# Scores of the last 64 queries of a head pair in four 64x64 tiles, with keys and values regrouped around their middle 64

## The chip, the cores and the metric

The kernel runs on one core of a Trainium2 chip. The metric is the time of one execution on the device in microseconds (us): the median of several runs.

## What is computed

Threshold attention over 8 batches, 8 heads, 576 positions and a head size of 64, followed by a Fourier mixing layer and a two-layer MLP with ReLU (512 to 2048 to 512). All data are 32-bit floats.

```python
scores = (1 / sqrt(64)) * q @ k.T                        # 8 x 8 x 576 x 576
thresh = max(scores, axis=-1) - tau
scores = where(scores >= thresh, scores, -1e9)
attn = exp(scores - max(scores, axis=-1))
attn = attn / (sum(attn, axis=-1) + 1e-9)
x = (attn @ v).transpose(0, 2, 1, 3).reshape(8, 576, 512)
u = x + real(fft(fft(x, axis=1), axis=2))
un = (u - mean(u)) / sqrt(var(u) + 1e-6)                 # over the last axis
out = u + maximum(un @ w_ch1, 0) @ w_ch2
```

## The kernel before

**Pairs and steps.** The 64 heads are worked on two at a time: 32 *pairs* n, four to a batch. The two heads of a pair lie above each other, head j = 0 on partitions 0 to 63, head j = 1 on 64 to 127. A pair has five *steps* t; the running number is i = 5n + t. In steps 0 to 3, 128 queries of each head are treated; in step 4, the *ends step*, the last 64 queries of both heads. 576 is four and a half times 128, so both queries and keys leave 64 over; that is what the change is about.

**Making ready.** `load_pair` loads q and k of a pair, `prep_pair` turns them in DVE's 32x32 transposes into `kT` and `qT` (64 rows of head size per head; lines 408, 409 and 411). `kT` has 64 columns in front that hold, for head 1 alone, its last 64 keys once more (L409), so that head 1 can read its keys rotated: the last 64 first, then 0 to 511. `scale_q` scales the raw q on ACT. `prep_ends` copies the last 64 query columns of both heads on GpSimd (L420) into `q_ends`, a 128x128 tile that is zero elsewhere: block-diagonal, head 0 in the first 64 rows and columns, head 1 in the others.

**Scores.** `scores(i)` writes into PSUM tiles `sc` of two banks each (two such tiles exist). In steps 0 to 3 each head has a tile with 288 keys in each bank; its matmuls use only the head's 64 rows of TensorE (64x128 tiles, L440), so the two heads can run beside each other. In the ends step two full-size matmuls (L446) of 128 rows with `q_ends` as the weights give one tile: 64 queries of head 0 on partitions 0 to 63 and of head 1 on the others, each against all 576 keys.

**Softmax.** DVE finds the row maximum, negated (`neg`, L461 in the first eight pairs, L520 later); ACT forms the exponential `e` (L477, L526) and the threshold `thr` (L530); DVE zeroes what lies under it and sums the rest (L540, denominators in `den_eps`); `inverse` adds up the denominators and takes the reciprocal (L385, L388). In an ends step all these are one instruction over 128 rows of 576 where the other steps need two. From pair 8 on ACT multiplies `e` with the reciprocal (L549); before that the reciprocals are carried along (`rec`, `spread_inverse`) and applied to the result of the values.

**Weights and values.** `weights_in_parts(i - 1)` transposes the previous step's `e` on TensorE and copies it out of PSUM on ACT. Columns 512 to 639 of `e` are the last 64 keys of head 0 followed by the last 64 keys of head 1: one 128x128 transpose (`pe`, L587) serves both, and goes to `ends` (L593; in an ends step two copies, L597). In the ends step, which has one head's width only, L504 or L554 first copies columns 512 to 575 to 576 to 639, so that both halves of the transpose hold them. The other 4 x 128 keys of each head are the transposes `pw` (L605) with copies to `e_t` (L607, L609). `values_in_parts` multiplies with v: five pairs of column-tiled matmuls (L636) into `pv`, four with `e_t`, the fifth with `ends`, whose v has zeros where the other head's keys stand. `load_v` brings v: `vt[:, 2c + j]` holds keys 128c to 128c + 127 of head j (c < 4), `vt[64j:64j+64, 8 + j]` its last 64, in four transfers on SP's queue.

**Three stretches.** Pairs 0 to 3 (`step`, with one `softmax` call per step; TensorE also prepares w1), pairs 4 to 7 (`second_batch`), and pairs 8 to 31 (the late loop), where a step's softmax is cut into `softmax_first`, `softmax_second` and `softmax_third` with pieces of the MLP and of the mixing of an earlier batch (`fill`, `mix`) between them. The order of each engine's instructions is what the program writes out, line by line. In the late loop it is, for an ends step: `scores` on TensorE; `softmax_first` (maximum, exponential, threshold); `fill`; `softmax_second` (mask, denominators); sometimes a part of the mixing; `weights_in_parts` of step 3; `fill`; `softmax_third`; `fill`; `load_pair`. `prep_pair` of the next pair stands at the end of step 3, just ahead of the ends step, and its transposes are thus ahead of the ends step's maximum on DVE. `prep_ends` stands at step 1, `load_v` at step 2.

**The work around it.** The MLP's two products are done by a two-level Strassen scheme: L1210 (first product, `ph`) and L1400 (second, `po`), 128x128 weights. L1147 and L1152 (DVE, ACT) evacuate `ph`, L1420 (DVE) adds `po` up, L1156, L1168, L1191, L1263 and L1346 are sums on GpSimd or DVE. The Fourier mixing of a batch: column sums and folds (L296, L299, L376), L766 (products `py`) with copies on ACT (L771, L776), L783 and L787 (products over the heads' dimension) into `f`. In the late loop it stands beside the first pair of the next batch. PSUM outside `sc` is a ring of four one-bank tiles (tag `mm`) that L1210, L1400, `pe`, `pw`, `pv` and `py` share in the order of the program: a tile comes free when its evacuation, on ACT or DVE, is done. w, hs and f are also moved to and from the device's main memory on SP's queue (L1074 among them), and L134 there loads q and k.

Of the kernel before, what the change touches and what calls it, by code (L numbers as in the profile page):

```python
# [9 lines left out]
FP32 = mybir.dt.float32  # L10
# [37 lines left out]
def kernel(  # L48
# [94 lines left out]
    def load_v(n):  # L143

        b, p = n // NPAIR, PAIRS[n % NPAIR]
        vt = v_in[n % 2]
        for j in range(2):
            h = 2 * p + (j + p) % 2
            nc.sync.dma_start(
                out=vt[:, j:8:2, :], in_=v[b, h, 0:512, :].rearrange("(t p) d -> p t d", p=128)  # L150
            )
            nc.sync.dma_start(out=vt[64 * j : 64 * j + 64, 8 + j, :], in_=v[b, h, 512:576, :])
# [15 lines left out]


    q_ends = const.tile([128, 128], FP32, name="q_ends")  # L170
    nc.gpsimd.memset(q_ends[:, :], 0.0)
# [211 lines left out]
    def inverse(i, nh):  # L383
        den = sb.tile([128, 2], FP32, tag="den", bufs=3, name="den")
        nc.vector.tensor_reduce(  # L385
            out=den[:, 0:nh], in_=den_eps[i % 3][:, 0:nh, :], axis=AXIS_X, op=ALU.add
        )
        nc.vector.reciprocal(den[:, 0:nh], den[:, 0:nh])  # L388
        return den

    heads = {}
    steps = {}
    xs = {}
# [7 lines left out]
    def prep_pair(n):  # L401
# [5 lines left out]
        kT = sb.tile([128, D + S], FP32, tag="kT", name="kT")  # L407
        nc.vector.transpose(kT[:, D : D + S], k_raw[:, :])
        nc.vector.transpose(kT[64:128, 0:D], k_raw[64:128, 512:S])  # L409
# [5 lines left out]

    def prep_ends(n):

        for j in range(2):
            hp = slice(64 * j, 64 * j + 64)
            nc.gpsimd.tensor_copy(q_ends[hp, hp], heads[n][0][hp, 512:S])  # L420
# [6 lines left out]
    def scores(i):  # L427
# [3 lines left out]
        nh = 2 if t < 4 else 1  # L431
        sc = [ps.tile([128, 2, 512], FP32, tag="sc", name=f"sc{j}") for j in range(nh)]
        if t < 4:
            order = [(c, j) for c in range(2) for j in range(2)]
            if i < per_batch:
                order.sort(key=lambda cj: cj[1])
            for c, j in order:
                if True:
                    hp, k0 = slice(64 * j, 64 * j + 64), D * (1 - j)
                    nc.tensor.matmul(  # L440
                        sc[j][:, c, 0:HALF], qT[hp, 128 * t : 128 * t + 128],
                        kT[hp, k0 + HALF * c : k0 + HALF * (c + 1)], start=True, stop=True,
                    )
        else:
            for c in range(2):
                nc.tensor.matmul(  # L446
                    sc[0][:, c, 0:HALF], q_ends[:, :], kT[:, D + HALF * c : D + HALF * (c + 1)],
                    start=True, stop=True,
                )
        steps[i] = (sc, nh)  # L450

    def softmax(i, between=None, meanwhile=None, behind=None):


        t = i % NT
        sc, nh = steps[i]
        neg = sb.tile([128, 2], FP32, tag="neg", bufs=3, name="neg")
        thr = sb.tile([128, 2], FP32, tag="thr", bufs=3, name="thr")
        e = sb.tile([128, 2 * S], FP32, tag="e", name="e")
        for j in range(nh):  # L460
            nc.vector.tensor_reduce(  # L461
                out=neg[:, j : j + 1], in_=sc[j][:, :, 0:HALF], axis=AXIS_XY, op=ALU.max,
                negate=True,
            )
        if meanwhile is not None:
            meanwhile()
        for j in range(nh):
            ej = e[:, S * j : S * (j + 1)].rearrange("p (c n) -> p c n", c=2)
            nc.scalar.activation(
                out=ej, in_=sc[j][:, :, 0:HALF], func=ACT.Exp, bias=neg[:, j : j + 1], scale=1.0  # L470
            )
            if j == 0:
                nc.scalar.activation(
                    out=thr[:, 0:nh], in_=neg[:, 0:nh], func=ACT.Identity,
# [1435 lines left out]
```

## Time and profile before

| What | us |
| --- | --- |
| median of 3 runs | 1545.07 (1543.23 to 1547.54) |
| the profiled execution: its own time | 1547.94 |
| its span, first to last instruction | 1546.2 |
| mean granted TensorE clock in it | 0.997 |

The profile is of one execution. Its busy times by stretch (us of the engine within each stretch; the first ends with pair 3, the second with pair 7, the third with pair 31, the last is the rest of the MLP):

| stretch, us | length | PE | DVE | ACT | POOL | DMA share |
| --- | --- | --- | --- | --- | --- | --- |
| 0 to 160 | 160 | 149.1 | 127.3 | 110.1 | 95.9 | 0.44 |
| 160 to 300 | 140 | 138.1 | 106.1 | 95.0 | 56.0 | 0.40 |
| 300 to 1340 | 1040 | 1036.1 | 718.0 | 655.7 | 514.6 | 0.52 |
| 1340 to 1546 | 206 | 200.6 | 111.7 | 55.6 | 112.8 | 0.58 |

PE is TensorE's matmuls, DVE VectorE, ACT ScalarE, POOL GpSimd, SP the engine that issues most transfers. Lines such as L446 are lines of the kernel. A line of the page's list of groups gives line, engine, operation, output<-input with sizes, count, then busy time, mean duration in ns, and the idle time just before such instructions with what ended most of it. Matmuls are pipelined and their ends are modelled, so that a matmul's duration contains time in which the one before it still ran: the distance between starts is the firmer number.

### The profile page before, as it was taken

To read this page: it belongs to the slowest core of one execution; us is meant where nothing else is said; L and a number is where in the kernel's file an instruction comes from. 1 tells how busy PE (TensorE), PEld (TensorE's weight loads), DVE (VectorE), ACT (ScalarE), POOL (GpSimd) and SP (SyncE) were. 2 spreads that over 40 slices of the span, in tenths; PEclk is the share of its full clock that TensorE was granted. 3 is DMA by queue.
4 is the path that set the end of the run, shared out by engine and by line. 5 is a ranking of instruction groups with operands and counts; after the bars stand their busy time and mean duration, and the time that the engine had idled before them with its cause. 6 is when DMAs were issued, how large, how long until landed. Compare 5 with 4: busy or idle time off the path is not lost.

```text
span 1546.2 us, 27021 instructions
## 1 busy us (share of the span) xinstructions
PE 1524.0 (99%) x9786; PEld 1186.0 (77%) x9786; DVE 1063.2 (69%) x2141; ACT 916.4 (59%) x1921; POOL 779.4 (50%) x964
## 2 busy tenths in 40 slices
PE   9999999999999999999999999999999999999999
PEld 5556555556788778887788878887788778989999
DVE  7977676846779466866578566956687657746546
ACT  6875676655666576656775666666665676133131
POOL 3775563034365642546255724554264625647635
PEclk9999999999999999999999999999999999999999
DMA  7423233465956354644455354635464534646655
GB/s 171 130 59 119 78 92 105 139 183 165 280 187 206 92 173 125 186 113 146 146 167 160 120 159 133 199 92 172 120 195 132 160 117 142 220 163 231 234 196 184
DMA packets 248907, 239.31 MB, mean 155 GB/s; under 512 B 197027, under 2 KB 218533, under 8 KB 228678
## 3 DMA queue, kind: packets, MB, share of 16 engines
q1 hardware_dynamic: 246262, 237.28, 50.1%
q8 instruction: 78, 1.28, 0.3%
q10 hardware_dynamic: 2512, 0.30, 0.1%
q14 instruction: 55, 0.45, 0.1%
HBM read 205.93 MB, written 31.46 MB: 154 GB/s over the span
## 4 chain that ended last, share of the span: by engine, by line
PE 91%; DVE 4%; ACT 2%; POOL 1%; DMA 1%; issue 0%; ACTq 0%; DVEq 0%; POOLq 0%
PE ph L1210 25%; PE po L1400 21%; PE pv L636 10%; PE sc L440 10%; PE pw L605 7%; PE po L933 4%; PE ph L909 3%; PE sc L446 2%; PE py L766 2%; PE pe L587 1%; PE pa L783 1%; PE pn L858 1%; PE pa L787 1%; PE pm L360 1%; PE po L1379 1%; DVE neg L461 1%
## 5 line engine op out<-in xcount | busy, mean ns | idle before, releaser
L520 DVE TENSOR_REDUCE neg<-sc 128x1 f32<-128x576 f32 x216 | 154.3, 751 | 117.1 <-PE sc L440 105.5
L526 ACT ACTIVATE e<-sc,neg 128x576 f32<-128x576 f32 x216 | 158.6, 734 | 114.3 <-DVE neg L520 114.3
L1147 DVE TENSOR_TENSOR hs<-ph,hs 128x512 f32<-128x512 f32 (+1 forms) x128 | 105.3, 823 | 167.1 <-PE ph L1210 97.3
L1400 PE MATMUL po<-w,w_all 128*128 128x128 f32 x1728 | 219.4, 276 | 0.0
L1400 PEld LDWEIGHTS po<-w,w_all 128*128 128x128 f32 x1728 | 205.4, 192 | 7.4 <-issue 4.0
L1156 POOL TENSOR_TENSOR w<-hs 128x512 f32<-128x512 f32 x32 | 42.1, 1317 | 312.3 <-ACT hs L1152 249.3
L540 DVE SCALAR_TENSOR_TENSOR e<-sc,thr,e 128x576 f32<-128x576 f32 x216 | 168.4, 812 | 27.2 <-ACT thr L530 27.1
L1210 PE MATMUL ph<-u_t,w 128*128 128x256 f32 x768 | 180.9, 382 | 0.6 <-DMA w<-f 0.6
L607 ACT COPY e_t<-pw 128x512 f32<-128x512 f32 x256 | 148.4, 594 | 44.2 <-PE pw L605 42.7
L440 PE MATMUL sc<-kT,qT 64*128 64x288 f32 x1024 | 168.4, 430 | 5.9 <-DVE e L477 5.5
L605 PE MATMUL pw<-ident,e 128*128 128x128 f32 x1152 | 169.3, 274 | 3.7 <-ACT ends L593 1.9
L549 ACT ACTIVATE e<-e,den 128x576 f32<-128x576 f32 x216 | 157.4, 774 | 2.9 <-DVE den L388 2.2
L1210 PEld LDWEIGHTS ph<-u_t,w 128*128 128x128 f32 x768 | 140.9, 190 | 23.6 <-issue 5.3
L1210 PE MATMUL ph<-w_all,w 128*128 128x256 f32 x672 | 157.1, 382 | 1.1 <-DVE w_all L1132 1.0
L605 PEld LDWEIGHTS pw<-ident,e 128*128 128x128 f32 x1152 | 135.8, 141 | 19.3 <-issue 5.6
L1263 POOL TENSOR_TENSOR w_all<-w_all 128x128 f32<-128x128 f32 (+2 forms) x160 | 121.7, 777 | 44.5 <-DVE w_all L1420 23.4
L1210 PEld LDWEIGHTS ph<-w_all,w 128*128 128x128 f32 x672 | 123.5, 190 | 23.9 <-issue 4.9
L1152 ACT ACTIVATE hs<-hs 128x512 f32<-128x512 f32 (+1 forms) x96 | 74.1, 772 | 113.8 <-DVE hs L1147 113.0
L440 PEld LDWEIGHTS sc<-kT,qT 64*128 64x128 f32 x1024 | 95.1, 186 | 55.4 <-issue 22.9
L1400 PE MATMUL po<-w,hs 128*128 128x128 f32 x912 | 119.8, 278 | 0.0
L1400 PEld LDWEIGHTS po<-w,hs 128*128 128x128 f32 x912 | 109.8, 192 | 9.5 <-issue 8.0
L636 PE MATMUL pv<-e_t,v_in 128*64 128x320 f32 (+1 forms) x512 | 72.1, 423 | 1.5 <-ACT e_t L609 0.8
(227 smaller groups left out, 2910.6 us busy)
## 6 DMA issues: line engine op xcount, KB each, us to landing
w<-f SPq DMA_DIRECT2D x150, 1024.0 KB, 4.9
hs<-in_moe_w_ch_dram SPq DMA_DIRECT2D x23, 512.0 KB, 4.7
q_in<-in_q_dram SPq DMA_DIRECT2D x128, 72.0 KB, 4.1
out_dram<-u SPq DMA_DIRECT2D x36, 256.0 KB, 2.5
k_in<-in_k_dram SPq DMA_DIRECT2D x124, 72.0 KB, 2.4
v_in<-in_v_dram SPq DMA_DIRECT2D x64, 128.0 KB, 5.1
f<-w SPq DMA_DIRECT2D x14, 512.0 KB, 3.3
f<-w SPq DMA_DIRECT2D x7, 1024.0 KB, 4.8
```

The costliest lines, as they stand in the source:

```text
L440: nc.tensor.matmul(sc[j][:, c, 0:HALF], qT[hp, 128 * t : 128 * t + 128], kT[hp, k0 + HALF * c : k0 + HALF * (c + 1)], start=True, stop=True,)
L520: nc.vector.tensor_reduce(out=neg[:, j : j + 1], in_=sc[j][:, :, 0:HALF], axis=AXIS_XY, op=ALU.max, negate=True,)
L526: nc.scalar.activation(out=ej, in_=sc[j][:, :, 0:HALF], func=ACT.Exp, bias=neg[:, j : j + 1], scale=1.0)
L540: nc.vector.scalar_tensor_tensor(out=ej, in0=sc[j][:, :, 0:HALF], scalar=thr[:, j : j + 1], in1=ej, op0=ALU.is_ge, op1=ALU.mult, accum_out ...
L549: nc.scalar.activation(out=e[:, S * j : S * (j + 1)], in_=e[:, S * j : S * (j + 1)], func=ACT.Copy, scale=den[:, j : j + 1],)
L605: nc.tensor.transpose(pw[:, c, :], e[:, c0 : c0 + 128], ident[:, :])
L607: nc.scalar.copy(e_t[:, 4 * j : 4 * j + 4, qs], pw[:, :, :])
L636: nc.tensor.matmul(pv[64 * j : 64 * j + 64, 0:m], vt[:, 2 * c + j, :], e_t[:, 4 * j + c, 0:m] if c < 4 else ends[:, 0, 0:m], start=(c == 0 ...
L1147: nc.vector.tensor_tensor(out=to, in0=bank, in1=to if other is None else other, op=ALU.add)
L1210: nc.tensor.matmul(bank[:, 256 * q : 256 * q + 256].rearrange("p (two n) -> p two n", two=2), left[:, 256 * c + 128 * q : 256 * c + 128 * ...
L1263: return lambda: eng.tensor_tensor(out=to, in0=to, in1=other, op=ALU.add)
L1400: nc.tensor.matmul(to, lefts[m][j][:, s], right_[:, 128 * s : 128 * (s + 1)], start=jn in (0, 4) and s == 0, stop=s == 3, skip_group_check ...
```

## The change

Three things, which go together:

- **The odd 64 keys are now those in the middle** (256 to 319) and no longer the last. `kT` is laid out as keys 256 to 575, 32 columns with a half of the middle 64 (another half for each head), then keys 0 to 319: 672 columns in four transposes. In steps 0 to 3 head 0 reads its keys as 320 to 575 and 0 to 319, head 1 as 256 to 575 and 0 to 255, cut into matmuls of 256 and 320 columns where both were 288; in PSUM the two pieces meet at the end of the first bank, so that the 576 are one run. The middle keys of both heads again stand beside each other in `e`, at 512 to 639. `load_v` brings the 512 other keys in two transfers for each head instead of one, and the middle 64 in a third.
- **The ends step's scores are four 64x64 tiles**: head j (rows of TensorE) times half c of its keys (columns, so partitions 64c to 64c + 63 of the output), 288 columns each; head j goes to bank j. `q_ends`, its memset and `prep_ends` are gone. Each row of the output now holds half the keys of one query of one head, in bank j.
- **The ends step's softmax follows that layout.** One maximum over both banks gives two numbers for each row (`own`); `exchange` copies them between the two halves of the partitions (two copies), and their minimum is `neg`. Exponential, mask and scaling are two instructions of 288 columns where one had 576; the denominators are exchanged between the halves as well, into a third column that `inverse` adds. `e` is 576 columns wide in that step; `pe` is the transpose of columns 256 to 383, and `ends` is filled by four copies of 32 partitions; `L504` and `L554` are gone.

The instructions that `softmax`, `softmax_first`, `softmax_second` and `softmax_third` had inline for the maximum, the exponential and the mask are moved into functions (`maxima`, `exponentials`, `masked`, `weights_of`).

```diff
@@ -146,10 +146,12 @@
         vt = v_in[n % 2]
         for j in range(2):
             h = 2 * p + (j + p) % 2
-            nc.sync.dma_start(
-                out=vt[:, j:8:2, :], in_=v[b, h, 0:512, :].rearrange("(t p) d -> p t d", p=128)
-            )
-            nc.sync.dma_start(out=vt[64 * j : 64 * j + 64, 8 + j, :], in_=v[b, h, 512:576, :])
+            for first, k0 in ((0, 320), (2, 0)):
+                nc.sync.dma_start(
+                    out=vt[:, first + j : 8 : 4, :],
+                    in_=v[b, h, k0 : k0 + 256, :].rearrange("(t p) d -> p t d", p=128),
+                )
+            nc.sync.dma_start(out=vt[64 * j : 64 * j + 64, 8 + j, :], in_=v[b, h, 256:320, :])
     tau_t = const.tile([128, 1], FP32, name="tau_t")
     nc.scalar.dma_start(out=tau_t[:, :], in_=tau.partition_broadcast(128))
...
-    q_ends = const.tile([128, 128], FP32, name="q_ends")
-    nc.gpsimd.memset(q_ends[:, :], 0.0)
...
@@ -380,16 +378,24 @@
     for den in den_eps:
         nc.vector.memset(den[:, :, :], 1e-9)
-    def inverse(i, nh):
+    den_ends = const.tile([128, 2, 3], FP32, name="den_ends")
+    nc.vector.memset(den_ends[:, :, :], 1e-9)
+    own = const.tile([128, 2], FP32, name="own")
+    other = const.tile([128, 2], FP32, name="other")
+
+    def inverse(i):
         den = sb.tile([128, 2], FP32, tag="den", bufs=3, name="den")
-        nc.vector.tensor_reduce(
-            out=den[:, 0:nh], in_=den_eps[i % 3][:, 0:nh, :], axis=AXIS_X, op=ALU.add
-        )
-        nc.vector.reciprocal(den[:, 0:nh], den[:, 0:nh])
+        parts = den_eps[i % 3]
+        if i % NT == 4:
+            parts = den_ends
+            exchange(parts[:, :, 2], parts[:, :, 0])
+        nc.vector.tensor_reduce(out=den[:, :], in_=parts[:, :, :], axis=AXIS_X, op=ALU.add)
+        nc.vector.reciprocal(den[:, :], den[:, :])
         return den
     heads = {}
     steps = {}
+    begun = {}
     xs = {}
     sums = {}
@@ -404,21 +410,18 @@
         q_raw, k_raw = loaded.pop(n)
-        kT = sb.tile([128, D + S], FP32, tag="kT", name="kT")
-        nc.vector.transpose(kT[:, D : D + S], k_raw[:, :])
-        nc.vector.transpose(kT[64:128, 0:D], k_raw[64:128, 512:S])
+        kT = sb.tile([128, S + 96], FP32, tag="kT", name="kT")
+        nc.vector.transpose(kT[:, 0:320], k_raw[:, 256:S])
+        nc.vector.transpose(kT[:, 352:672], k_raw[:, 0:320])
+        for j, k0 in ((0, 288), (1, 256)):
+            hp = slice(64 * j, 64 * j + 64)
+            nc.vector.transpose(kT[hp, 320:352], k_raw[hp, k0 : k0 + 32])
         qT = sb.tile([128, S], FP32, tag="qT", bufs=1, name="qT")
         nc.vector.transpose(qT[:, :], q_raw[:, :])
         heads[n] = (qT, kT, v_in[n % 2])
         if n + 1 < B * NPAIR and not late:
             load_pair(n + 1)
-    def prep_ends(n):
-
-        for j in range(2):
-            hp = slice(64 * j, 64 * j + 64)
-            nc.gpsimd.tensor_copy(q_ends[hp, hp], heads[n][0][hp, 512:S])
-
     def normalized(n):
-        sc = [ps.tile([128, 2, 512], FP32, tag="sc", name=f"sc{j}") for j in range(nh)]
+        sc = [
+            ps.tile([128, 2, 512], FP32, tag="sc", name=f"sc{j}") for j in range(2 if t < 4 else 1)
+        ]
+        order = [(c, j) for c in range(2) for j in range(2)]
+        if i < per_batch and t < 4:
+            order.sort(key=lambda cj: cj[1])
+        for c, j in order:
+            hp = slice(64 * j, 64 * j + 64)
+            if t < 4:
+                k0, k1 = ((64, 320), (352, 672), (0, 320), (352, 608))[2 * j + c]
+                to = sc[j][:, c, 512 - (k1 - k0) : 512] if c == 0 else sc[j][:, c, 0 : k1 - k0]
+                q_cols = slice(128 * t, 128 * t + 128)
+            else:
+                k0, k1 = ((64, 352), (352, 640), (32, 320), (320, 608))[2 * j + c]
+                to, q_cols = sc[0][64 * c : 64 * c + 64, j, 0:HALF], slice(512, S)
+            nc.tensor.matmul(
+                to, qT[hp, q_cols], kT[hp, k0:k1], start=True, stop=True, skip_group_check=t == 4
+            )
         if t < 4:
-            order = [(c, j) for c in range(2) for j in range(2)]
-            if i < per_batch:
-                order.sort(key=lambda cj: cj[1])
-            for c, j in order:
-                if True:
-                    hp, k0 = slice(64 * j, 64 * j + 64), D * (1 - j)
-                    nc.tensor.matmul(
-                        sc[j][:, c, 0:HALF], qT[hp, 128 * t : 128 * t + 128],
-                        kT[hp, k0 + HALF * c : k0 + HALF * (c + 1)], start=True, stop=True,
-                    )
+            steps[i] = [
+                sc[j][:, :, :].rearrange("p c n -> p (c n)")[:, 256 - 64 * j : 832 - 64 * j]
+                for j in range(2)
+            ]
         else:
-            for c in range(2):
-                nc.tensor.matmul(
-                    sc[0][:, c, 0:HALF], q_ends[:, :], kT[:, D + HALF * c : D + HALF * (c + 1)],
-                    start=True, stop=True,
+            steps[i] = [sc[0][:, j, 0:HALF] for j in range(2)]
+
+    def weights_of(i, e, j):
+
+        if i % NT == 4:
+            return e[:, HALF * j : HALF * (j + 1)]
+        return e[:, S * j : S * (j + 1)]
+
+    def maxima(i):
+        neg = sb.tile([128, 2], FP32, tag="neg", bufs=3, name="neg")
+        sc = steps[i]
+        if i % NT < 4:
+            for j in range(2):
+                nc.vector.tensor_reduce(
+                    out=neg[:, j : j + 1], in_=sc[j], axis=AXIS_X, op=ALU.max, negate=True
                 )
-        steps[i] = (sc, nh)
+            return neg
+        both = bass.AP(
+            tensor=sc[0].tensor, offset=sc[0].offset,
+            ap=[list(sc[0].ap[0]), [512, 2], list(sc[0].ap[1])],
+        )
+        nc.vector.tensor_reduce(
+            out=own[:, :], in_=both, axis=AXIS_X, op=ALU.max, negate=True
+        )
+        exchange(other[:, :], own[:, :])
+        nc.vector.tensor_tensor(out=neg[:, :], in0=own[:, :], in1=other[:, :], op=ALU.min)
+        return neg
+
+    def exchange(out_, in_):
+
+        for half in range(2):
+            a, b = 64 * half, 64 - 64 * half
+            nc.vector.tensor_copy(out_[a : a + 64], in_[b : b + 64])
+
+    def exponentials(i, e, neg, thr, j):
+        nc.scalar.activation(
+            out=weights_of(i, e, j), in_=steps[i][j], func=ACT.Exp, bias=neg[:, j : j + 1],
+            scale=1.0,
+        )
+        if j == 0:
+            nc.scalar.activation(
+                out=thr[:, :], in_=neg[:, :], func=ACT.Identity, bias=thr_off[:, :], scale=-1.0
+            )
+
+    def masked(i, e, thr, j):
+        ej = weights_of(i, e, j)
+        nc.vector.scalar_tensor_tensor(
+            out=ej, in0=steps[i][j], scalar=thr[:, j : j + 1], in1=ej, op0=ALU.is_ge,
+            op1=ALU.mult, accum_out=(den_ends if i % NT == 4 else den_eps[i % 3])[:, j, 0:1],
+        )
     def softmax(i, between=None, meanwhile=None, behind=None):
-        t = i % NT
...
     def spread_inverse(i):
         e, den = steps[i]
-        if i % NT == 4:
-            nc.scalar.copy(e[:, S : S + 64], e[:, 512:S])
         if den is None:
             return
-        nh = den.shape[1]
+        nc.scalar.copy(rec[:, :].rearrange("p (j d) -> p j d", j=2), _repeated(den, D))
...
     def softmax_first(i):
+        neg = maxima(i)
...
+        for j in range(2):
+            exponentials(i, e, neg, thr, j)
...
     def softmax_second(i):
...
+        e, thr = begun.pop(i)
+        for j in range(2):
+            masked(i, e, thr, j)
+        steps[i] = (e, inverse(i))
...
     def softmax_third(i):
...
-        if nh == 1:
-            nc.scalar.copy(e[:, S : S + 64], e[:, 512:S])
+        e, den = steps[i]
+        for j in range(2):
+            ej = weights_of(i, e, j)
+            nc.scalar.activation(out=ej, in_=ej, func=ACT.Copy, scale=den[:, j : j + 1])
...
-        nc.tensor.transpose(pe[:, 0, :], e[:, 512:640], ident[:, :])
+        c0 = 512 if t < 4 else 256
+        nc.tensor.transpose(pe[:, 0, :], e[:, c0 : c0 + 128], ident[:, :])
         kept = 1
...
             for j in range(2):
-                hp = slice(64 * j, 64 * j + 64)
-                nc.scalar.copy(ends[hp, 0:kept, q0 : q0 + 64], pe[hp, 0:kept, hp])
+                for half in range(2):
+                    p0 = 64 * j + 32 * (1 - half)
+                    nc.scalar.copy(
+                        ends[p0 : p0 + 32, 0, q0 : q0 + 64],
+                        pe[32 * j : 32 * j + 32, 0, 64 * half : 64 * half + 64],
+                    )
+            if kept == 2:
+                nc.scalar.copy(ends[:, 1, q0 : q0 + 64], pe[:, 1, 0:64])
         qs = slice(q0, q0 + (128 if t < 4 else 64))
         for j in range(2 if t < 4 else 1):
             pw = ps.tile([128, 4, 128], FP32, tag="mm", bufs=4, name="pw")
             if j == 1:
                 yield
             for c in range(4):
-                c0 = (S + D) * j + 128 * c
+                if t < 4:
+                    c0 = (S + D) * j + 256 * (c % 2) + 128 * (c // 2)
+                else:
+                    c0 = 320 * (c // 2) + 128 * (c % 2)
                 nc.tensor.transpose(pw[:, c, :], e[:, c0 : c0 + 128], ident[:, :])
             if t < 4:
                 nc.scalar.copy(e_t[:, 4 * j : 4 * j + 4, qs], pw[:, :, :])
             else:
                 nc.scalar.copy(
-                    e_t[:, :, qs].rearrange("p (j c) q -> p j c q", j=2),
-                    pw[:, :, :].rearrange("p c (j q) -> p j c q", j=2),
+                    e_t[:, :, qs], pw[:, :, :].rearrange("p c (two q) -> p (c two) q", two=2)
                 )
     def values_in_parts(n, part):
...
-        if t == 1:
-            prep_ends(n)
         if i > 0:
             transposed_weights(i - 1)
         spread_inverse(i)
```

The calls of `prep_ends` in the other two stretches go as well.

## The prediction

> **What bounds the kernel now.** I read the page's busy shares and its chain first, then the timeline of TensorE around each kind of score step, then, for every place where TensorE resumes after a score step of a pair's last 64 queries (an "ends step", 32 of them), what it waits for and since when that was ready.
>
> ```profile
> PE 1524.0 (99%) x9786; PEld 1186.0 (77%) x9786; DVE 1063.2 (69%) x2141; ACT 916.4 (59%) x1921; POOL 779.4 (50%) x964
> ...
> PE 91%; DVE 4%; ACT 2%; POOL 1%; DMA 1%; issue 0%; ACTq 0%; DVEq 0%; POOLq 0%
> PE ph L1210 25%; PE po L1400 21%; PE pv L636 10%; PE sc L440 10%; PE pw L605 7%; PE po L933 4%; PE ph L909 3%; PE sc L446 2%; PE py L766 2%; PE pe L587 1%; PE pa L783 1%; PE pn L858 1%; PE pa L787 1%; PE pm L360 1%; PE po L1379 1%; DVE neg L461 1%
> ```
>
> TensorE is the bound from about 200 us on; the other engines only matter where TensorE has to wait for them. The ends step's matmuls (L446) are 2% of the chain, about 31 us: all that this change can save on TensorE lies in there. DVE's 4% lies mostly in the first 160 us, where the chain through that stretch gives L461 5.8% and L477 4.3%.
>
> ```profile
> 903.83 1.89 PE L1210 MATMUL ph<-u_t,w 128*128 128x256 f32 x8
> 905.65 1.24 PE L440 MATMUL sc<-kT,qT 64*128 64x288 f32 x8
> 906.83 1.99 PE L1210 MATMUL ph<-u_t,w 128*128 128x256 f32 x8
> 908.65 0.27 PE L587 MATMUL pe<-ident,e 128*128 128x128 f32 x1
> ...
> 914.36 1.95 PE L636 MATMUL pv<-e_t,v_in 128*64 128x256 f32 x16
> 916.14 0.60 PE L636 MATMUL pv<-ends,v_in 128*64 128x256 f32 x4
> 916.67 0.48 PE L1210 MATMUL ph<-w_all,w 128*128 128x256 f32 x1
> ...
> 922.51 0.59 PE L1210 MATMUL ph<-w_all,w 128*128 128x256 f32 x2
> 922.94 1.13 PE L446 MATMUL sc<-kT,q_ends 128*128 128x288 f32 x4
> 923.91 0.38 PE L1210 MATMUL ph<-u_t,w 128*128 128x256 f32 x1
> ```
>
> Columns: start, us, engine, line. Every f32 matmul is two passes. Starts, not durations, are to be read. Plain 256-column passes follow each other by 0.43/2 = 0.215 us (922.51 to 922.94). The ends step takes 923.91 - 922.94 = 0.97 us, four passes of 288 columns at 0.243, with full-size neighbours on both sides and no gap.
>
> **TensorE's part.** After the change the step is four 64x64 tiles of two passes each. The other tiled groups show what a change of tiling costs. Entering: eight passes from 903.83 take 1.82 where 8 x 0.215 = 1.72, so 0.10. Leaving: the eight from 906.83 take 1.82 too, 0.10. Inside: the 20 column-tiled passes from 914.36 to 916.67 take 2.31, and ten rounds of two at once 2.15, so 0.16 (their weights are 64 wide, as the new ones are; the 128-wide ones of L440 lose 1.18 - 4 x 0.243 = 0.21). Row pairs (905.65) and column pairs (914.36) both run at once, so I let all four tiles run at once: two rounds, 0.49 + 0.36 = 0.85 instead of 0.97. The gain is 0.12 to 0.13 us a pair, 32 x 0.13 = 4.2 us at most. If only two tiles ran at once: 0.97 + 0.36, a loss of 0.36.
>
> The Trainium skill speaks against four at once: "TensorE: Matmul & The Clock Gate", Part 3, says that a weight load overlaps running matmuls only where the row group differs, and the two column tiles of a head share theirs. By that rule the step would be the pairwise one, a loss. In this trace the column pairs of L636 share their row group and do overlap, so I take the rows.
>
> The scores of the other steps keep their 1152 columns, cut 256/320 instead of 288/288: each head still has 576 and the heads run beside each other (905.65). I take 0; the bounds are 0 and one difference of a pass, (320 - 288) x 0.00084 = 0.03 us, on 128 steps: 3 us.
>
> **DVE's part, each pair.** Transposes: L408 is 774 ns for 576 columns, L409 242 for 64, so some 1.04 ns a column and 0.18 fixed: two of 320 (0.51 each) and two of 32 (0.21) replace 774 + 242: 1.44 - 1.02 = +0.42. Two copies and a min stand between the row maximum and the exponential; no copy of this size is in the trace. Bounds: 0.06 (the 128x1 memset of L173) and 1.50 (one L299 beside GpSimd's L376, where it is 0.42 alone). I take 0.16, as L385 and L388 (157 and 166 ns, chained at 0.19): +0.50 for the three. The mask as two of 288: a second fixed part, +0.17. Two copies ahead of the denominators: +0.34. Sum 1.4 us of 69% busy DVE.
>
> **ACT's part.** Two exponentials of 288 for one of 576: +0.10; the scaling likewise +0.10; the copy L554/L504 (0.24 to 0.27) goes; four `ends` copies for two (L597, 0.21 each): +0.43, and a fifth in pairs 0 to 7, for the reciprocals. **GpSimd** loses two copies of 0.27 (L420). **SP** issues six loads of v for four, some 0.5 us each, into a queue that itself waits 395 us for L1400; between stores and weight loads I count 0, at worst 1 us on one step of the first batch, 4 us.
>
> **Where the delay reaches TensorE.** The transposes and the exchange stand one after the other on DVE's queue ahead of the exponential, which ACT runs ahead of copies that free PSUM. Whether this costs depends on the margin at each place.
>
> ```profile
> 840.40 0.74 DVE L520 TENSOR_REDUCE neg<-sc 128x1 f32<-128x576 f32 x1
> 841.07 0.67 DVE L1420 TENSOR_TENSOR w_all<-w_all,po 128x512 f32<-128x512 f32 x1
> ...
> 841.24 0.74 ACT L526 ACTIVATE e<-sc,neg 128x576 f32<-128x576 f32 x1 [1.62 <-DVE neg L520]
> ...
> 842.14 0.63 ACT L771 COPY y_o<-py 48x256 f32<-48x256 f32 x1
> ...
> 842.82 0.94 PE L766 MATMUL py<-dim_c,f 128*128 128x65 f32 x6
> ```
>
> This is the step of pair 20, the first pair of a batch, beside the Fourier products: L771 ends at 842.77 and L766 starts 0.05 later. DVE was busy without a pause from the transposes to L520, so the maximum comes 0.42 later, the exchange adds 0.50, ACT then holds L771 back to 843.1: TensorE loses 0.95 net. Pairs 12, 20, 24 and 28 repeat this (3.8 us). Pair 16 has 0.5 us of margin: +0.5. Pair 8 has DVE idle before the maximum: no loss. At 410.79 (pair 10) L1210 starts 0.06 after L1147, which stands behind the maximum on DVE: +0.93. At 717.21 (pair 17) L1210 starts 0.05 after L593 behind the exponential: +0.7. The other 17 pairs from 8 on have margins above the delay (at 928.35 L1210 starts 1.00 after L593, of which 0.5 goes; at 968.77 it is 0.64 of which 0.2 goes): they keep the gain, 17 x -0.13 = -2.2. Late pairs: 3.8 + 0.5 + 0.9 + 0.7 - 2.2 = +3.7.
>
> Second batch (pairs 4 to 7): TensorE stood 0.18 after L504, which goes; against it L636 stands 0.07 to 0.50 after L609, which three more `ends` copies, 0.64, push back by 0.64 - 0.27 = 0.37. Those 0.37 less the 0.18 are 0.2; two of the four pairs have the small margin: +0.4.
>
> First batch: DVE is busy 36 of the 40 us from 40 to 80. Pair 0: the next maxima have 0.8 us of idle DVE ahead, of 1.4: +0.55. Pair 1 has 0.2: +1.3. Pair 2 has 2 us: 0. Pair 3: L636 starts 0.05 after L609: +0.7. Sum +2.5.
>
> GpSimd works in the place of the exchange in pairs 12, 20, 24 and 28 (an L1191 from 841.67, 1.28 us). The copies resemble L296 and L299 (one input, SBUF to SBUF) more than L385, and those wait out GpSimd's instruction. I count half of it: 4 x 0.6 = +2.4.
>
> The skill's "SBUF — State Buffer" states such a lock of the port pair between the two engines, with the loser blocked for the whole instruction; by it these four places would cost 1.2 us each instead of 0.6.
>
> Sum: 3.7 + 0.4 + 2.5 + 2.4 = +9.0 us. The profiled execution took 1547.94 (span 1546.2), 0.2% above the median of 1545.07; the difference is put on the median: 1554.1.
>
> **Rivals.**
> - All of it hidden: margins absorb the delays, TensorE keeps 4.2 us: 1540.9. For: 17 late pairs have room, DVE is 69% busy. Against: the 0.05 us margins above, and DVE at 90% from 40 to 80.
> - Tiles run two at a time: 0.36 + 0.13 more on the 21 pairs that were to gain or stay even, +10: 1564. For: no four at once in this trace. Against: both kinds of pairs run at once.
> - DVE's small instructions wait for GpSimd everywhere (the slower side's own mechanism; it decides once each costs over 0.6): 0.6 more on four pairs, 1.0 on the four like pair 23 (L1168 from 966.55 in the exchange's place), 1.5 in the first batch: +8, 1562.
> - Half of the delays are absorbed, with no GpSimd waits: the 3.7 + 0.4 + 2.5 = 6.6 halved: 1545.07 + 3.3, 1548.
>
> **How the numbers follow.** Main case 0.45 (own range 1549 to 1558), hidden 0.17, pairwise 0.12, GpSimd everywhere 0.16, half 0.10. The time is the main case's. 0.3% is 4.6 us, about what a measurement here can tell from no change: faster means under 1540.4, slower over 1549.7. Hidden lies at the edge, and TensorE's gain could be larger than 0.13 if the switches of tiling cost less here than in the rows: 0.09 faster, 0.08 within. Half gives 0.07 within, the main case 0.03. So 0.09, 0.18, 0.73. Range 1544 to 1563: below it most of the hidden case, above it half of the pairwise one.
>
> **What would show it.** Four starts within 0.03 us at the new score line, and 0.85 us to the next matmul: right; 1.3: pairwise. The copies of the exchange at 0.16, or at 1 us beside GpSimd. At the first pair of the batches from 12 on, the matmul after y_o some 1 us later, ended by ACT. The late plain pairs 0.13 us shorter. I am wrong if the first 160 us don't grow, if the margins hold, or if the unequal cuts cost on all 128 steps.

## The result, and the profile after

The changed kernel takes 1600.89 us (median of 4 runs, 1600.57 to 1601.04) against 1545.66 before: 55.2 us more, a ratio of 1.0359 with a 95% interval of 1.0345 to 1.0372. The forecast was 1554.1, its range 1544 to 1563. The sign was right, the size was not: six times the forecast loss.

The page of the changed kernel, busy shares and the chain that ended last:

```profile
PE 1539.9 (96%) x9914; PEld 1191.7 (75%) x9914; DVE 1126.6 (70%) x2430; ACT 928.3 (58%) x2017; POOL 756.8 (47%) x899
...
PE 74%; DVE 14%; ACT 7%; DMA 3%; issue 1%; SPq 1%; POOL 0%; ACTq 0%; DVEq 0%
PE ph L1232 22%; PE po L1422 17%; PE pv L658 9%; PE sc L449 9%; PE pw L628 5%; PE po L955 3%; ACT e L493 3%; DVE e L504 2%; PE ph L931 2%; DVE qT L420 1%; DVE other L490 1%; DVE own L479 1%; PE py L788 1%; PE pa L805 1%; DVE hs L1169 1%
```

TensorE's part of the chain fell from 91% to 74%, and what came in is DVE (14% for 4%) and ACT (7% for 2%), among it the lines of the new ends step: L490 is the exchange, L479 its maximum, L493 holds the exponentials (of all steps), and L420 is the transposition of the *next* pair's q, which the change doesn't touch. (Most lines behind the score functions are 22 higher than before: L1232 was L1210, L1422 was L1400, L1169 was L1147, L1213 was L1191.)

TensorE itself got what was forecast. The timeline of TensorE at the ends step of pair 22, the place shown for before:

```profile
961.17 1.67 PE L1232 MATMUL ph<-w_all,w 128*128 128x256 f32 x7
962.77 0.71 PE L449 MATMUL sc<-kT,qT 64*64 64x288 f32 x8
963.42 1.78 PE L1232 MATMUL ph<-u_t,w 128*128 128x256 f32 x7
```

Between the eight passes of the group the records have two sets of four starts, each set within 0.02 us, 0.29 apart: all four tiles run at once. The seven plain passes ahead of the group would end, at 0.216 a pass, 7 x 0.216 = 1.51 after 961.17, at 962.68; the second plain pass behind it starts at 963.74 (its record), so that 963.74 - 0.216 - 962.68 = 0.84 us belong to the step, 0.13 less than the 0.97 of before. The four starts lie within 0.02 us in all 32 pairs.

The loss is made elsewhere. The chain of waits through the same step of pair 14, a late pair far from any mixing, where before the kernel ran without a gap (start, us, what):

```profile
613.24 0.69 PE sc L449 x8
613.93 0.02 issue
613.95 0.78 DVE qT L420
614.73 1.11 DVE hs L1169
615.84 0.68 DVE own L479
...
616.91 0.17 DVE neg L483
...
618.24 0.52 ACT hs L1174
618.76 0.16 ACT ends L607
618.92 0.04 issue
618.97 1.99 PE ph L1232 x8
```

The chain leaves TensorE at the new scores and comes back 5.0 us later. In between TensorE works on what is ready and stands idle for only 0.45 us, just ahead of 618.97; the whole pair takes 0.62 us more than before. DVE starts on qT only when the scores are done. `qT` has a single buffer; before, the ends step read a copy (`q_ends`), so the next pair's transposition could run ahead of the ends step's scores. Now these read `qT` itself, and the transposition, which stands ahead of everything else on DVE's queue, waits for them. Behind it come the evacuation L1169, the maximum, the exchange, ACT's exponentials, and only then the copy (L607) that frees the tile for TensorE. The group list has the sum of that wait (count, then busy time and mean ns, then idle time ahead and what ended it):

```profile
L420 DVE STREAM_TRANSPOSE qT<-q_in 128x576 f32<-128x576 f32 x32 | 24.9, 778 | 31.7 <-PE sc L449 31.3
```

31.3 us of DVE standing still. Before, this transposition (L411) had an idle time of 1.0, and in pair 14 it began ahead of the ends step's scores (L446):

```profile
L411 DVE STREAM_TRANSPOSE qT<-q_in 128x576 f32<-128x576 f32 x32 | 24.9, 778 | 1.0
...
584.91 0.78 DVE L411 STREAM_TRANSPOSE qT<-q_in 128x576 f32<-128x576 f32 x1
585.46 1.13 PE L446 MATMUL sc<-kT,q_ends 128*128 128x288 f32 x4
```

The second thing is the exchange. In pair 20, the first pair of a batch (the place of the prediction's last timeline):

```profile
876.94 1.27 POOL L1213 TENSOR_TENSOR w_all<-hs,w_all 128x512 f32<-128x512 f32 x1 [1.34 <-issue]
877.09 1.32 DVE L490 COPY other<-own 64x2 f32<-64x2 f32 x2
...
878.52 0.69 DVE L1442 TENSOR_TENSOR w_all<-w_all,po 128x512 f32<-128x512 f32 x1
...
879.26 0.66 PE L628 MATMUL pw<-ident,e 128*128 128x128 f32 x4 [1.63 <-DVE w_all L1442]
```

Two copies of two columns take 1.32 us; they end 0.2 us after GpSimd's instruction (878.21). L1442, which frees a PSUM tile, stands behind them, and TensorE waits 1.63 us for it. All such waits of the transposes together, before (where the lines were L605 and L1420) and after (in total, times, longest, us):

```profile
PE pw L605 <- DVE w_all L1420: 0.2, 1, 0.2
...
PE pw L628 <- DVE w_all L1442: 6.9, 5, 1.6
```

Where the time went, by the start of pair 8's scores in the profiles (275.0 us before): the changed kernel is 17.0 us late there, and 36.1 more are lost from there to the end of the span. Of the late pairs the five that are first of a batch from 12 on lose 1.7 to 5.1 each, pair 11 2.4, and most plain ones, which were to *gain* 0.13, lose 0.6 (nine of them) to 1.6. All such splits come from one execution each.

### The profile page after: what moved, and what is told of

It reads as the page before. It is cut to its first block, busy times and chain, and to the rows that moved or that the text cites. A ratio compares the mean times of both kernels' runs of the same rounds, so it can differ in the third digit from the quotient of the medians.

```text
span 1599.2 us, 27673 instructions
## 1 busy us (share of the span) xinstructions
PE 1539.9 (96%) x9914; PEld 1191.7 (75%) x9914; DVE 1126.6 (70%) x2430; ACT 928.3 (58%) x2017; POOL 756.8 (47%) x899
## 4 chain that ended last, share of the span: by engine, by line
PE 74%; DVE 14%; ACT 7%; DMA 3%; issue 1%; SPq 1%; POOL 0%; ACTq 0%; DVEq 0%
PE ph L1232 22%; PE po L1422 17%; PE pv L658 9%; PE sc L449 9%; PE pw L628 5%; PE po L955 3%; ACT e L493 3%; DVE e L504 2%; PE ph L931 2%; DVE qT L420 1%; DVE other L490 1%; DVE own L479 1%; PE py L788 1%; PE pa L805 1%; DVE hs L1169 1%
## 5 line engine op out<-in xcount | busy, mean ns | idle before, releaser
L493 ACT ACTIVATE e<-sc,neg 128x576 f32<-128x576 f32 (+1 forms) x320 | 219.7, 687 | 194.0 <-DVE neg L471 122.2
L504 DVE SCALAR_TENSOR_TENSOR e<-sc,thr,e 128x576 f32<-128x576 f32 (+1 forms) x320 | 229.7, 753 | 47.1 <-ACT thr L498 25.3
L471 DVE TENSOR_REDUCE neg<-sc 128x1 f32<-128x576 f32 x256 | 181.7, 750 | 107.1 <-PE sc L449 106.9
L1422 PE MATMUL po<-w,w_all 128*128 128x128 f32 x1728 | 222.0, 278 | 2.5 <-ACT ends L607 2.3
L1422 PEld LDWEIGHTS po<-w,w_all 128*128 128x128 f32 x1728 | 206.8, 193 | 12.2 <-issue 6.2
L449 PE MATMUL sc<-kT,qT 64*128 64x320 f32 (+2 forms) x1280 | 196.2, 431 | 12.5 <-DVE e L504 12.1
L1169 DVE TENSOR_TENSOR hs<-ph,hs 128x512 f32<-128x512 f32 (+1 forms) x128 | 104.9, 819 | 138.1 <-PE ph L1232 70.1
L1232 PE MATMUL ph<-u_t,w 128*128 128x256 f32 x768 | 182.9, 384 | 5.9 <-ACT ends L607 5.1
L628 PE MATMUL pw<-ident,e 128*128 128x128 f32 x1152 | 171.2, 276 | 12.6 <-DVE w_all L1442 6.9
L567 ACT ACTIVATE e<-e,den 128x576 f32<-128x576 f32 (+1 forms) x240 | 161.7, 725 | 18.0 <-DVE den L393 18.0
L449 PEld LDWEIGHTS sc<-kT,qT 64*128 64x128 f32 (+1 forms) x1280 | 118.4, 176 | 65.4 <-issue 36.0
L1232 PEld LDWEIGHTS ph<-u_t,w 128*128 128x128 f32 x768 | 140.1, 190 | 33.9 <-ACT ends L607 7.7
L628 PEld LDWEIGHTS pw<-ident,e 128*128 128x128 f32 x1152 | 136.4, 143 | 30.0 <-DVE w_all L1442 7.9
L1232 PE MATMUL ph<-w_all,w 128*128 128x256 f32 x672 | 157.2, 382 | 1.1 <-DVE w_all L1154 1.0
L1232 PEld LDWEIGHTS ph<-w_all,w 128*128 128x128 f32 x672 | 123.3, 190 | 24.3 <-issue 6.8
L1422 PE MATMUL po<-w,hs 128*128 128x128 f32 x912 | 120.8, 279 | 1.8 <-ACT w_all L1434 1.8
L1422 PEld LDWEIGHTS po<-w,hs 128*128 128x128 f32 x912 | 109.3, 192 | 13.5 <-issue 9.7
```

Of the source, the lines that this page charges most:

```text
L449: nc.tensor.matmul(to, qT[hp, q_cols], kT[hp, k0:k1], start=True, stop=True, skip_group_check=t == 4)
L471: nc.vector.tensor_reduce(out=neg[:, j : j + 1], in_=sc[j], axis=AXIS_X, op=ALU.max, negate=True)
L493: nc.scalar.activation(out=weights_of(i, e, j), in_=steps[i][j], func=ACT.Exp, bias=neg[:, j : j + 1], scale=1.0,)
L504: nc.vector.scalar_tensor_tensor(out=ej, in0=steps[i][j], scalar=thr[:, j : j + 1], in1=ej, op0=ALU.is_ge, op1=ALU.mult, accum_out=(den_en ...
L567: nc.scalar.activation(out=ej, in_=ej, func=ACT.Copy, scale=den[:, j : j + 1])
L628: nc.tensor.transpose(pw[:, c, :], e[:, c0 : c0 + 128], ident[:, :])
```

## Experiments

Three causes were to be told apart: the wait for `qT` (31.3 us of DVE), the exchange beside GpSimd, and the longer chain as such. The exchange's copies and the minimum behind them, in the changed kernel:

```profile
L490 DVE COPY den_ends<-den_ends 64x2 f32<-64x2 f32 x64 | 32.2, 503 | 1.5
L490 DVE COPY other<-own 64x2 f32<-64x2 f32 x64 | 22.3, 348 | 1.5
```

128 copies with a median of 0.165 us would take 21.1; they took 54.5, 33.4 more.

**1. The wait for qT removed.** The last 64 query columns are copied once more, into a tile of their own, in the places where `prep_ends` had stood (this and the following edits in extracts):

```diff
+        nc.gpsimd.tensor_copy(q_last[:, :], heads[n][0][:, 512:S])
...
-                to, qT[hp, q_cols], kT[hp, k0:k1], ...
+                to, (qT if t < 4 else q_last)[hp, q_cols], kT[hp, k0:k1], ...
```

> The changed kernel, but the last 64 query columns are copied on GpSimd (one 128x64 copy at step 1, where before had two 64x64 copies) and the ends step's scores read that copy, so that the next pair's qT transposition need not wait for them. Theory A (most of the 55 us come from DVE standing at that transposition, 31.3 us over 22 pairs, and from exchange copies beside GpSimd, 33.4 us above 0.165 us each): DVE's idle time ahead of the qT transposition falls to under 3 us, and the time by 20 to 30 us, to 1571 to 1581. Theory B (the longer chain of instructions as such, the split masks, exponentials and ends copies): the wait of DVE goes, but the time falls by less than 6, 1595 or more.

Measured: 1588.47 (ratio 1.0280, 1.0258 to 1.0303), 12.4 less. DVE's idle time ahead of the transposition fell from 31.7 to 1.1. The nine plainest late pairs turned from a loss of 0.6 to a gain of 0.1 to 0.3, while pairs 24 and 28 lose 1.6 more each than in the changed kernel (the clock, see the end). So the wait is real and costs what such pairs lost, but 12.4 is under theory A's 20 and over theory B's 6: neither number held.

**2. The exchange by another operation.**

```diff
-            nc.vector.tensor_copy(out_[a : a + 64], in_[b : b + 64])
+            nc.vector.tensor_reduce(out=out_[a : a + 64], in_=one, axis=AXIS_X, op=ALU.max)
```

(`one` is the same input with a last axis of length 1.)

> The changed kernel with the exchange's four copies a pair made by tensor_reduce over one element instead of tensor_copy. The row of L392 (a tensor_reduce, 156 to 159 ns in all 128) says that this operation does not wait for GpSimd. Theory A: each of the 128 instructions takes 0.16 us instead of 0.43 on average, 33 us of DVE's time go, half or somewhat less of it on the path: 1581 to 1591. Theory B: 1597 or more. If reduces wait for GpSimd too: durations up to 1.28 stay, 1600.

Measured: 1590.66 (1.0293, 1.0278 to 1.0309), 10.2 less, just inside theory A's interval. The groups in that run:

```profile
L483 DVE TENSOR_TENSOR neg<-own,other 128x2 f32<-128x2 f32 x32 | 10.5, 329 | 1.1
L494 DVE TENSOR_REDUCE den_ends<-den_ends 64x2 f32<-64x2 f32 x64 | 9.7, 151 | 1.5
```

No reduce waits: all 128 lie between 148 and 153 ns, and 66 of them ran beside an instruction of GpSimd. But the minimum L483 behind them, 168 ns on average in the changed kernel, is at 329 now, 1.27 us at worst: the wait moved one instruction on.

**3. Both edits.**

> Both edits together. Theory A: 1552 to 1562, what is left being the split instructions and the exchange's fixed parts, less TensorE's 0.13 a pair. Theory B: 1590 or more. If the two delays cover each other (either alone stalls TensorE), the gain of both is more than the sum of the two alone.

Measured: 1572.65 (1.0185, 1.0167 to 1.0203), 28.2 less, where the two alone make 12.4 + 10.2 = 22.6: the two delays cover each other in part. Theory A's 1552 to 1562 was missed by 11 us; something else was left.

**4. No exchange at all.** The copy of q stays, the exchange and the minimum are left out: each row keeps the maximum and the denominator of its own half of the keys, so the last 64 queries get another result.

```diff
-        exchange(other[:, :], own[:, :])
-        nc.vector.tensor_tensor(out=neg[:, :], in0=own[:, :], in1=other[:, :], op=ALU.min)
-        return neg
+        return own
...
-            exchange(parts[:, :, 2], parts[:, :, 0])
```

> As the first, and the exchange is left out altogether: each row keeps the maximum and the denominator of its own half of the keys, so the outputs of the last 64 queries are another function. Against both edits together it shows what the seven small instructions (four exchanges, one minimum, at 0.16 us each, and their place in the chain) still cost: theory A 3 to 8 us less than that run, 1546 to 1556; if small instructions without a lock cost nothing, the same as that run within 2 us.

Measured: 1551.46 (1.0042, 1.0027 to 1.0057). The exchange with its minimum still cost 21.2 us in the run of both edits, not 3 to 8. From pair 8 to the end this run loses 0.3 us against before: without an exchange the tiles cost nothing there, but they don't gain 24 x 0.13 = 3.1 either, since four of the pairs that are first of a batch and pair 10 give back 0.3 each and the end of the loop 1.6.

**5. The minimum by a reduce too.** `own` and `other` lie beside each other in one tile.

```diff
+        nc.vector.tensor_reduce(out=neg[:, :], in_=both_max[:, :, :], axis=AXIS_X, op=ALU.min)
```

> As both edits together, and the minimum too is a tensor_reduce (own and other lie beside each other and are reduced with min) instead of a tensor_tensor, which beside GpSimd took up to 1.03 us in the run of both edits (mean 0.377 against 0.160 alone). Theory C (what is left above the run without an exchange, 21 us, is the minimum's wait for GpSimd, 7 us of DVE's time at places where ACT and TensorE stand behind it): 1552 to 1558. Theory D (the length of the exchange's chain itself, some 0.8 us between maximum and exponential): 1565 to 1573, as both edits together.

Measured: 1564.62 (1.0126, 1.0109 to 1.0143), 8.0 less than with both edits, and 13.2 more than without an exchange. The minimum, from the groups of this run:

```profile
L489 DVE TENSOR_REDUCE neg<-both_max 128x2 f32<-128x4 f32 x32 | 5.0, 157 | 1.1
```

That is just under theory D's 1565 to 1573 and far over theory C's 1552 to 1558, but both had a part: the minimum's wait is 8.0 of the 21.2 (C), the chain without any wait 13.2 (D).

**6. The wait for qT, with no lock.** As the fifth, without the copy of q.

> The changed kernel with exchange and minimum as tensor_reduce, but without the copy of q, so that the next pair's qT transposition waits for the ends step's scores as in the change. Against the run without any lock it gives the price of that wait alone. Theory A: 10 to 16 us more than that run, 1564 to 1572. If the wait only hurts together with the locks: the same within 4.

Measured: 1580.60 (1.0231, 1.0217 to 1.0245), 16.0 more than the fifth, at the upper edge of what was expected (the time itself is over the expected 1564 to 1572, because the fifth came out slower than assumed there). 11.6 of the 16.0 by which the spans differ arise from pair 8 on: 0.7 in each of the plainest pairs (+0.4 to +0.6 here, -0.3 to -0.1 in the fifth). The 4.4 before pair 8 are not waits of TensorE, which is idle there for 20.3 us here and 20.7 in the fifth; in these two executions the clock withheld 5.1 us more of full-speed time (12.0 against 6.8: half of the time at half clock).

**7. The regrouping alone**, with the ends step of before.

```diff
+        if heads_of(i) == 1:
+            for c in range(2):
+                k0 = (32, 352)[c]
+                nc.tensor.matmul(
+                    sc[0][:, c, 0:HALF], q_ends[:, :], kT[:, k0 : k0 + HALF], start=True, stop=True
+                )
```

> The regrouping alone, with the ends step as before (block-diagonal q, two full-size matmuls over keys 288 to 575 and 0 to 287, one softmax over 576; the middle keys reach the 128x128 transpose by two ACT copies instead of one): kT in four transposes, v in six transfers, scores of steps 0 to 3 cut 256/320. The prediction gave the regrouping +0.42 us of DVE a pair and 0 to 3 us for the unequal cuts. Theory: 0 to +3, 1545 to 1549. If the unequal cuts or the loads of v cost on every step: 1550 or more.

Measured: 1548.06 (median of 11 runs; 1.0018, 1.0009 to 1.0027), 2.3 more than before, within the expected 0 to 3. Four transposes, two more loads of v and the unequal cuts are nearly free. In its profile it reaches pair 8 2.7 us *earlier* than before, where the clock was at half for 3.4 us and before for 10.2: that much a split at pair 8 of single executions can be off.

**8. Tiles from pair 8 on**, with the exchange by reduces, the earlier pairs as in the seventh.

> Pairs 0 to 7 with the ends step as in the run of the regrouping alone, pairs 8 to 31 with four 64x64 tiles (their queries from the block-diagonal copy, whose filled blocks are the 64x64 weights) and the exchange without a lock. Theory C: TensorE gains 0.13 to 0.2 us on each of 24 pairs, 3 to 5 us, from the time of the regrouping alone: 1541 to 1545. Theory D: the chain costs in the late pairs, 1555 or more.

Measured: 1551.64 (1.0046, 1.0033 to 1.0058), 3.6 *more* than the seventh. By the starts of the pairs in the two profiles, 8 and before, fifteen of the seventeen pairs from 9 to 30 that are not first of a batch gain 0.1 each, but pairs 12, 16, 20, 24 and 28 lose 0.6 to 1.2, pair 10 0.7, pair 17 0.3, and the last 1.1: together more than the gain. Theory C fails, theory D's 1555 is not reached.

**9 and 10. Half of the exchange.** The fifth without the exchange of the maxima, and without that of the denominators; the last 64 queries again get another result.

> As the run without any lock, but the maxima are not exchanged (three small instructions between maximum and exponential go; each half row uses its own maximum, so the last 64 queries are another function); the denominators still are. The exchange's chain as a whole cost 13 us (1564.6 against 1551.5). Theory E: the place counts, not the number; the maxima's part stands ahead of the exponential, which ACT runs ahead of the copies of the Fourier products, so it holds most: 9 to 12 of the 13 go, 1552 to 1556. Theory F: DVE's time counts as such, three of five instructions: 8 go in all stretches alike, about 1557.

> As the run without any lock, but the denominators are not exchanged (two small instructions between mask and reciprocal go; the last 64 queries are another function). Theory E: 1 to 4 go, all of them before pair 8, 1560.5 to 1563.5, and the late pairs that are first of a batch still lose 0.7 to 1. Theory F: 5 go, 1559.5.

Measured: 1552.62 (1.0052, 1.0038 to 1.0066) and 1562.81 (1.0115, 1.0100 to 1.0131): the three instructions of the maxima cost 12.0 us, the two of the denominators 1.8. These runs come from another round than the fifth, in which the kernel before had 1544.72 where it had 1545.80; taken from the kernel before of each round, it is 10.9 and 0.7. The denominators' part can't be told from nothing: the intervals of the tenth and the fifth run overlap. The 5 us that theory F expected for it are out. The place decides (theory E): what stands ahead of the exponential delays ACT's queue and with it the copies out of PSUM. That the denominators' part would arise before pair 8 alone did not hold: of the 6.4 us by which the two spans differ (single executions, of which the medians keep 1.8), 4.1 arise before pair 8 and 2.3 behind it.

**11. Tiles only where they gained**, pairs from 8 on that are not first of a batch, without 10 and 31; their q from `q_ends`.

> Four 64x64 tiles and the lock-free exchange only in the 17 pairs from 8 on in which the runs so far kept TensorE's gain (not the first pair of a batch, not pairs 10 and 31); the other pairs have the ends step as in the run of the regrouping alone. Those 17 pairs gained 0.1 us each, net of what comes back between their other steps: 1548.1 less 1.7, about 1546.4, which is no better than before. If the gain is the full 0.2 seen behind the ends step: 1544.7.

Measured: 1547.36 (11 runs; 1.0016, 1.0007 to 1.0025). Against the regrouping alone it is 0.7 better, which the intervals don't tell from nothing, and it is not better than before. (That makes 16 pairs, not the 17 of the expectation, and pair 17, which lost 0.3 in the eighth run, is among them.) By the starts of the pairs, 14 of the 16 gain 0.1 to 0.5 against the seventh run, but 17 and 18 lose 0.3 and 0.2, and pairs 16, 24, 28 and 31, whose own ends step is that of before, 0.6 each. No version here beats the kernel before.

## Why the prediction was right in sign and wrong in size

The runs take the 55.2 us apart, in the order in which they were taken off (the terms of the first two depend on that order; together they are 36.3):

| Part | us | from |
| --- | --- | --- |
| exchange and minimum waiting for GpSimd | 20.3 | 1600.9 - 1580.6 (23.9 with the q copy: 1588.5 - 1564.6) |
| next pair's qT waiting for the scores | 16.0 | 1580.6 - 1564.6 (12.4 with the locks: 1600.9 - 1588.5) |
| exchange as a chain, no waits | 13.2 | 1564.6 - 1551.5; 10.9 to 12.0 of it the maxima |
| split masks and exponentials, `ends` copies, less TensorE's gain | 3.4 | 1551.5 - 1548.1 |
| regrouping | 2.3 | 1548.1 - 1545.8 |

Each term holds what the clock did in its runs. The sign did not hang on the two waits: with both removed the fifth run is still 18.8 us slower than before, and 1564.62 is over the range's end of 1563.

- **TensorE's part** held: 0.84 against 0.85, four tiles at once. The rival of pairwise tiles is out. The rule that the prediction set against it, from the Trainium skill's "TensorE: Matmul & The Clock Gate", Part 3, that a weight load overlaps running matmuls only where the row group differs, does not fit these records: the four starts are 7 ns apart, in the program's order 13 ns for two tiles of the same row group, and in pair 22 the weight loads of the second four passes are recorded from 962.83 to 962.98, while the first four (from 962.77) still run in both row groups.
- **The unequal cuts and the transposes** held: from the first pass to the next work 1.17 us (945.39 to 946.56) where it was 1.18, and the regrouping as a whole 2.3.
- **The step that failed first** is "GpSimd loses two copies of 0.27 (L420)". It counted the copies as work that goes and did not ask what they released. They had freed `qT`, which has one buffer, some steps ahead of the ends step. Nothing in the prediction has a term for that wait; it is worth 12 to 16 us (11.6 of the 16.0 from pair 8 on), and it fell on the plain late pairs that were to keep a gain of 2.2.
- **GpSimd's part** was the right mechanism, in the main case with half its price in four pairs (2.4) and as a rival with 8. It measured 20 to 24. One delay was counted at a place where up to five instructions can wait (four copies, and the minimum, which nobody had on the list), and the places were not only the four: against the sixth run, pairs 11, 17 and 19 of the changed kernel lose 1.1 to 2.1 more, 12 and 20 4.2 and 2.7, 24 and 28 1.0 each. The path was another too: at the first pair of a batch the prediction let ACT hold y_o back, and TensorE waits 0.41 us for that, but 1.63 for L1442, which stands behind the exchange on DVE's own queue. The nearest rows chosen for the copies, L385 and L388, are a reduce and a reciprocal; the reduces here never waited. The bound of 1.50 from L299 had been the right end.
- **The delay chain** (+3.7 late, +2.9 earlier) is the fifth run: 8.8 from pair 8 on and 11.0 before it, in its profile. The late places were the right ones: pairs 12 and 20 lose 0.8 and 0.9, 24 and 28 1.9 each (0.95 written for each of the four), 10 0.7 (0.93), 16 1.1 (0.5); pair 17 loses 0.1 (0.7). In pair 20 of that run half of it comes by the path that was written (0.41 for y_o), half by DVE's queue (0.45 for L1442's line). Missed were pair 8 (1.3) and the end of the loop (2.3). Before pair 8 the sum was a quarter of what came: TensorE stands idle there for 20.7 us where it was 12.8, and the clock withholds 6.8 us where it was 5.1, which the prediction has no term for. It put 0 on pair 2 and hardly anything on pairs 4 to 7; pairs 2 and 6 lose 4.7 and 5.2 in that profile, of which 3.4 and 1.7 are the clock's (pair 3 gains 1.8, 1.7 of it the clock's).

## What to carry to other kernels

A copy that a change makes superfluous may be what lets a buffer go: look for the next writer of the tile that the consumer now reads directly, and for where that writer stands in its queue. A swap between halves of the partitions costs little in busy time and much by its place: three instructions of 0.16 us ahead of an exponential cost 11 to 12 us over 32 pairs, two behind it at most 2. Where GpSimd works beside them, small DVE instructions with their data in SBUF should take a form that doesn't wait for it, here a reduce.

## What the runs showed of the hardware

**Which DVE operations wait for GpSimd.** On 64x2 and 128x2 operands in SBUF: copies 161 ns at least and up to 1.50 us (first run), a tensor_tensor with two inputs 160 ns up to 1.27 us, reduces 148 to 153 ns in all 128 (second run). What they wait for shows in the ends: in the changed kernel all 49 copies that took over 0.22 us end 21 to 29 ns after the end of an instruction of GpSimd. The Trainium skill's "SBUF — State Buffer", Who interferes with whom, says the same of all three: copies can contend with GpSimd, instructions with two inputs from SBUF do where GpSimd reads SBUF, and a tensor_reduce on trn2 never does. This case's rows agree.

**A clock drop makes such a stall dearer.** The stall of pair 12, in windows of 2 us of the changed kernel (PE, PEld, DVE, ACT and POOL busy, granted clock, DMA share, GB/s):

```profile
526.00:528.00 2.00, 0.59 (x5) 0.22 (x2) 1.95 (x4) 0.32 (x1) 1.17 (x1) 1.00 0.80 131
528.00:530.00 2.00, 1.36 (x8) 1.12 (x8) 1.33 (x7) 1.82 (x6) 0.00 (x0) 0.71 0.87 140
530.00:532.00 2.00, 2.00 (x10) 2.00 (x11) 0.84 (x4) 0.79 (x3) 0.00 (x0) 0.50 0.02 3
```

TensorE was busy for 1.95 of 4 us, and its clock was 0.50 from some 528.8 on; it is 0.58 in the window from 534 to 536 and 1.00 from there, with TensorE busy without a pause from 530. Four pairs have the same stall, TensorE waiting 1.63 us for L1442 and 0.41 for y_o: 12, 20, 24 and 28. In 12 and 20 the clock fell (0.60 and 0.54 in the windows from 880 to 884), and they lost 5.1 and 4.6 us; in 24 and 28 it did not, and they lost 2.9 each. So the clock's answer to one stall was worth about 2 us, and came or not. In the profile of the first run it came in 20, 24 and 28, which lost 4.6 us each. The mean granted clock of the whole run is 0.990 against 0.997 before; 1599.2 x 0.010 - 1546.2 x 0.003 = 11 us more of full-speed time withheld, some of it while TensorE had to wait anyway. The skill's "TensorE: Matmul & The Clock Gate", What's actually happening, has the clock at half after one idle window of some 3.4 us. Here TensorE was not idle for that long in one piece: its longest gap was 1.63 us, though from 526.3 to 529.3 it had nothing but the transposes L601 and L628. The same stretch in pairs 24 and 28 left the clock alone; what decides is not shown.
